# Zero matmuls between the first tiles, a new order of the first loads, and a third PSUM bank for the last gate/up units

## The chip, the cores and the metric

The kernel runs on one core of one Trainium2 chip. The metric is the device time of one execution in microseconds (us); lower is better. Five engines work side by side, each through its own instructions in order: PE (TensorE, the matmuls), ACT (ScalarE), DVE (VectorE), POOL (GpSimd) and SP (SyncE, which here only issues DMAs). They wait for each other and for DMAs through semaphores.

## The reference

A token matrix `x` (2048 x 512, bfloat16) is normalised by rows, and two branches of the result are added to `x`:

```python
xn  = (x - mean) / sqrt(var + 1e-5)                 # by row
# A: linear attention, 32 heads of 16
q, k, v = split(xn @ wqkv)                          # 512 -> 3 * 512
phi(p)  = concat(softmax(p @ w_phi), softmax(-p @ w_phi))     # 16 -> 32 per head
kv = sum_s phi(k)[s]^T v[s];  z = sum_s phi(k)[s]
o  = phi(q) @ kv / (phi(q) @ z + 1e-6)
# B: gated branch, F = 1792
h  = (xn @ w_gate) * (xn @ w_up)
out = x + o @ wo + h @ w_down
```

## The kernel before

The 2048 tokens are 16 tiles of 128 rows. `D = 512` is four blocks of 128 (`NQ`), `F = 1792` is fourteen (`NF`).

**The stages.** For each tile, `emit_ln_stats` (lines 407 to 420) takes mean and variance on DVE (`bn_stats` L410, `bn_aggr` L412), adds epsilon (L417, on DVE for tiles 0 to 3, on POOL for the others), and raises to the power -0.5 on POOL (L419). `emit_xn` (line 433) makes the normalised tile on DVE (L434) and transposes it into `xnT`: for tiles 0 to 3 with four PE matmuls against an identity and an ACT copy (L443, recorded as the helper's L277), for tiles 4 to 15 with a DMA transpose on SP. `k_pe(t)` multiplies a tile by the V weights, `wprime` builds the products W' of the K or Q weights with the feature matrix (its POOL part is `make_wbd`, L392), `k_pk(t)` and `k_norm(t)` make the softmax features of K, `emit_kv` sums K features times V, and `q_pk`, `q_scale`, `q_T` (a DMA transpose), `q_num` (eight narrow matmuls and a division) and `q_oT` (a DMA transpose) do the Q side of one tile. A GLU unit `glu(g, ft)` handles four tiles `g` and one of the fourteen blocks `ft`: four matmuls of 512 columns for the gate into one PSUM bank, four for up into another, an ACT copy of the gate (L543) and a DVE product (L545). There are 56 units; the last nine or ten run among the Q stage. `final(t)` sums 18 matmuls into one bank (the down projection and the attention output), DVE adds `x` (L642), and SP stores the tile.

**Loads.** All come from SP, in the order of the code at lines 352 to 361: tiles 0, 1, 2 and 3 of `x`; the V weights; tiles 4 to 7 of `x`; gate and up columns of blocks 0 to 3; `w_phi`; the K weights, transposed (`load_wT(1, ...)`); gate and up columns of blocks 4 to 13 as one load each, with rows of 2560 bytes. Later loads wait for an earlier DMA.

**Start.** DVE writes a zero tile (L365), and PE runs 46 matmuls of 128 columns on it (line 366) before anything else.

**The order.** The code records steps (`_Sched.step`, `_Sched.dma`) with what they read and write. `_order` (line 732) then plays the steps through with a cost for each, and at each point takes the step that can start first, by priority among those that can start at once. For a load it takes the time `at` as its landing; for a transpose on SP it takes `land` after the start of the issue. The result is one fixed order per engine; the hardware waits for the real semaphores (`_emit_all`). So a changed cost, `at` or `land` changes no instruction, but can change the order on every engine. Every recorded matmul has line L297, every ACT step L277, plain DMAs L165 and DMA transposes L164.

**Banks.** PSUM has eight banks of 512 columns. `a_banks` rotates those of the tile products, `glu_banks` those of the GLU units: (5, 6, 7) first, (4, 5, 6, 7) later, (5, 6) for the last units, and then `final` uses 7 for tiles 0 to 3 and 7, 5, 6 in rotation after that (line 715).

Of the kernel before, what the change touches and what calls it, by code (L numbers as in the profile page):

```python
# [12 lines left out]
PE, ACT, DVE, POOL, SP = "PE", "ACT", "DVE", "POOL", "SP"  # L13
# [7 lines left out]
NQ = D // 128  # L21
# [176 lines left out]
def _build(nc, es, A_x, A_wqkv, A_w_phi, A_wo, B_w_gate, B_w_up, B_w_down, out):  # L198
# [59 lines left out]
    def sbv(name, lo, n):  # L258
        off = layout[name] + lo
        return arena[:, off:off + n]  # L260
# [5 lines left out]
    def bank(b, lo=0, n=512):  # L266
        return psum[:, b * 512 + lo: b * 512 + lo + n]

    sc = _Sched(nc)


    def act_op(out_ap, in_ap, func=ACTF.Copy, scale=1.0, bias=None, prio=None):
        def fn(e):
            kw = {}
            if bias is not None:
                kw["bias"] = bias
            return e.activation(out=out_ap, in_=in_ap, func=func, scale=scale, **kw)  # L277
        r = [in_ap]
        if isinstance(scale, bass.AP):
            r.append(scale)  # L280
        if isinstance(bias, bass.AP):
            r.append(bias)
        return sc.step(ACT, fn, reads=r, writes=[out_ap], cost=(50.0 if str(in_ap.tensor.name) == "ps" else 95.0) + 0.833 * in_ap.free_size(),
                       lat=180.0, prio=prio)

    def dve(fn, reads, writes, n, rate=1.0, fixed=65.0, prio=None):
        return sc.step(DVE, fn, reads=reads, writes=writes, cost=fixed + rate * n / 0.96, lat=150.0, prio=prio)
# [1 line left out]
    def pool(fn, reads, writes, n, rate=1.8, fixed=130.0, prio=None):  # L289
        return sc.step(POOL, fn, reads=reads, writes=writes, cost=fixed + rate * n, lat=120.0, prio=prio)  # L290

    def mms(items, prio=None, warm=False):

        def fn(e):
            ins = None
            for o, l, r, a, z in items:
                ins = e.matmul(o, lhsT=l, rhs=r, start=a, stop=z)  # L297
            return ins
        reads = []
        writes = []  # L300
        c = 0.0
        for o, l, r, a, z in items:
            reads += [l, r]
            writes.append(o)
            c += max(25.0, o.free_size() / 2.4 + 2.3) * (1.6 if warm else 1.0)
        return sc.step(PE, fn, reads=reads, writes=writes, cost=c, lat=260.0, prio=prio)

    def group(o, pairs):
# [3 lines left out]
    ident = sbv("ident", 0, 128)  # L312
# [6 lines left out]
    def x_tile(t):  # L319
        return sbv("x", t * 512, 512)  # L320
# [7 lines left out]
    wv_v = sbv("wv", 0, NQ * 512).rearrange("p (q j) -> p q j", q=NQ)  # L328
# [7 lines left out]
    def load_x(on, t0, n, at):  # L336
        return sc.dma(on, sbv("x", t0 * 512, n * 512).rearrange("p (t d) -> p t d", t=n),
                      x_flat[t0 * 128:(t0 + n) * 128, :].rearrange("(t p) d -> p t d", p=128), at=at)

    def load_w(on, dst, src, at, issue=500.0):  # L340
        return sc.dma(on, dst, src, at=at, issue=issue)

    def load_wT(w, at):

        return sc.dma(SP, wT_v[:, w, :, :], A_wqkv[:, w * 512:(w + 1) * 512], transpose=True, at=at, issue=4600.0)

    def load_gu(on, f0, n, at):
        return [load_w(on, v[:, :, f0 * 128:(f0 + n) * 128],
                       src[:, f0 * 128:(f0 + n) * 128].rearrange("(q p) f -> p q f", p=128), at)
                for v, src in ((wg_v, B_w_gate), (wu_v, B_w_up))]  # L350

    load_x(SP, 0, 1, 3150.0)
    load_x(SP, 1, 1, 3700.0)
    load_x(SP, 2, 2, 4800.0)
    load_w(SP, wv_v, A_wqkv[:, 1024:1536].rearrange("(q p) j -> p q j", p=128), 6800.0)
    load_x(SP, 4, 4, 8200.0)
    load_gu(SP, 0, 4, 10800.0)
    sc.dma(SP, wphi_v, bass.AP(tensor=A_w_phi.tensor, offset=A_w_phi.offset, ap=[[16, 128], [2048, NQ], [1, 16]]),
           at=12500.0)
    load_wT(1, 14500.0)  # L360
    load_gu(SP, 4, 10, 20500.0)


    zero = sbv("tree", 0, 128)
    dve(lambda e: e.memset(zero, 0.0), [], [zero], 128)  # L365
    mms([(bank(7, 0, 128), zero, zero, True, True)] * 46, warm=True)


    def c_fn(e):
# [52 lines left out]
    def xn_tile(t):  # L422
        return sbv("xn", (t % 4) * 512, 512)
# [4 lines left out]
    def next_a():  # L428
        b = a_bank[0] % a_banks[0]
        a_bank[0] += 1  # L430
        return b

    def emit_xn(t):
        dve(lambda e: e.tensor_scalar(out=xn_tile(t), in0=x_tile(t), scalar1=mv_v[:, t, 0:1],  # L434
                                      scalar2=rstd_v[:, t, 0:1], op0=ALU.subtract, op1=ALU.mult),
            [x_tile(t), mv_v[:, t, 0:1], rstd_v[:, t, 0:1]], [xn_tile(t)], 512, rate=0.5)
        if t >= 4:
            sc.dma(SP, xnT_v[:, :, t * 128:(t + 1) * 128], xn_tile(t), transpose=True, issue=1250.0, land=3200.0,
                   at=36000.0 + 1300.0 * (t - 8) if t >= 8 else 22500.0 + 1300.0 * (t - 4))
            return  # L440
        b = next_a()
        mms([(bank(b, q * 128, 128), xn_tile(t)[:, q * 128:(q + 1) * 128], ident, True, True) for q in range(NQ)])
        act_op(xnT_v[:, :, t * 128:(t + 1) * 128], bank(b).rearrange("p (q s) -> p q s", q=NQ))  # L443


# [106 lines left out]
    def emit_kv(half):  # L552
        for g in range(8):
            b = next_a()
            mms(group(bank(b, 0, 65), [(ek_v[:, t, g * 128:(g + 1) * 128], vext_all[:, t, g, 0:65])
                                       for t in range(half * 8, half * 8 + 8)]))
            kp = kvp_v[:, g, :]
            if half == 0:
                act_op(kp, bank(b, 0, 65))
                continue  # L560
            dve(lambda e, b=b, kp=kp: e.tensor_tensor(out=kp, in0=bank(b, 0, 65), in1=kp, op=ALU.add),  # L561
                [bank(b, 0, 65), kp], [kp], 65)
            dve(lambda e, kp=kp, g=g: e.tensor_tensor(
                out=kvx_v[:, g, 0:64].rearrange("p (h d) -> p h d", h=4),
                in0=kp[:, 0:64].rearrange("p (h d) -> p h d", h=4),
                in1=maskh[:, :, None].to_broadcast([128, 4, 16]), op=ALU.mult),
                [kp, maskh], [kvx_v[:, g, 0:64]], 64)
            dve(lambda e, kp=kp, g=g: e.scalar_tensor_tensor(
                out=kvx_v[:, g, 64:68], in0=maskh, scalar=kp[:, 64:65], in1=eps4, op0=ALU.mult, op1=ALU.add),
                [kp, maskh, eps4], [kvx_v[:, g, 64:68]], 4)  # L570


    oT_v = sbv("oT", 0, NQ * S_TOK).rearrange("p (q s) -> p q s", q=NQ)
# [7 lines left out]
    def eq(t):  # L581
        return sbv("eq", (t % 3) * 1024, 1024)

    def eT(t):
        return sbv("eT", (t % 3) * 1024, 1024).rearrange("p (g s) -> p g s", g=8)
# [16 lines left out]
                                      op=ALU.mult), [e1, rs], [e1], 512, rate=0.5)  # L602

    def q_T(t):
        sc.dma(SP, eT(t), eq(t), transpose=True, issue=1250.0, land=3300.0)

    nd = psum[:, 3 * 512:5 * 512].rearrange("p (g k) -> p g k", g=8)

# [11 lines left out]

    def q_oT(t):
        o = sbv("oring", (t % 2) * 512, 512)
        sc.dma(SP, oT_v[:, :, t * 128:(t + 1) * 128], o, transpose=True, issue=1250.0, land=3200.0)


    out_ctr = [0]
# [21 lines left out]
    glu_banks = [(5, 6, 7)]  # L648

    def load_later(*loads):  # L650

        queued = sc.by_eng[SP][-1]
        for load in loads:
            load().deps.append(queued)

    def some_glu(n, g_max):
        for _ in range(n):
            if units and units[0][0] <= g_max:
                glu(*units.pop(0), glu_banks[0])

    def ln(t0, n):
        emit_ln_stats(t0, n)
        for t in range(t0, t0 + n):
            emit_xn(t)
# [9 lines left out]
    for b0 in range(0, NT, 4):  # L674
        if b0 == 4:
            a_banks[0] = 4
            glu_banks[0] = (4, 5, 6, 7)
        if b0 < 12:
            ln(b0 + 4, 4)
        if b0 == 0:  # L680
            load_later(lambda: load_x(SP, 8, 8, 29000.0))
        if b0 == 4:
            load_later(lambda: load_w(SP, wd_v, B_w_down.rearrange("(f p) j -> p f j", p=128), 48000.0),
                       lambda: load_w(SP, wo_v, A_wo.rearrange("(q p) j -> p q j", p=128), 50000.0))
        if b0 == 8:
            load_wT(0, 0.0).deps.append(sc.by_eng[SP][-2])
            emit_kv(0)
            some_glu(99, 2)
        for t in range(b0, b0 + 4):
            k_pk(t)  # L690
            k_norm(t)
            if b0 < 8:
                some_glu(2, 1)
        if b0 < 12:
            for t in range(b0 + 4, b0 + 8):
                k_pe(t)
        if b0 == 8:
            some_glu(4, 3)
            wprime(0)
    emit_kv(1)  # L700
    glu_banks[0] = (5, 6)
    some_glu(99, 3)
    LEAD = 2
    for t in range(NT + LEAD + 1):
# [165 lines left out]
```

## Time and profile before

| | us |
|---|---|
| median of 3 runs | 223.19 (222.98 to 223.47) |
| the profiled execution | 222.43 |
| its span, first to last instruction | 220.7 |
| PE busy in it | 215.4 (98%) |
| DVE busy | 192.8 (87%) |
| ACT busy | 114.4 (52%) |
| POOL busy | 9.6 (4%) |

The lines of a timeline have the start, the length, the engine, the source line, what is written from what, the number of instructions merged into the line and, in brackets, the idle time of the engine before them with what ended it. In the chain of waits each line is a piece of the path that ended last: start, length, who. In a table of stretches the columns are the stretch, its length, PE's busy time with the number of matmuls touched, the granted TensorE clock, the busy share of the DMA engines and GB/s. "PEld" is PE loading a stationary operand. The ends of matmuls are modelled, so neighbouring matmuls overlap in the profile; the spacing of their starts is the real rate.

### The profile page before, as it was taken

How to read it: one execution, taken by the hardware profiler on the slowest of the kernel's cores; microseconds unless marked ns; L12 is line 12 of the kernel's file. 1: busy time of each engine (PE TensorE's matmuls, PEld its weight loads, DVE VectorE, ACT ScalarE, POOL GpSimd, SP SyncE). 2: the span in 40 equal slices, each digit the busy share in tenths (PEclk: the TensorE clock that was granted, in tenths of full speed). 3: DMA queues.
4: the chain of work that ended last, by engine and by line, in shares of the span. 5: the costliest groups of instructions: out<-in, count | busy, mean ns of one | idle time of the engine just before them, and what ended most of it. 6: DMA issues, size and time to landing. Idle time of an engine off the chain costs nothing.

```text
span 220.7 us, 3555 instructions
## 1 busy us (share of the span) xinstructions
PE 215.4 (98%) x1273; PEld 107.0 (48%) x1296; DVE 192.8 (87%) x552; ACT 114.4 (52%) x189; POOL 9.6 (4%) x25
## 2 busy tenths in 40 slices
PE   8899999999999999999999999999999999999995
PEld 8454444444445545444445544444445454444544
DVE  5855999999998289999999999999999999998421
ACT  2668977466442699875543676656454433230000
POOL 4250000200003000000000000000000000000000
PEclk9999999999999999999999999999999999999999
DMA  6999720139200340000000004435446556565621
GB/s 175 324 295 287 177 80 3 25 74 337 88 3 19 77 95 3 0 0 0 3 0 1 3 0 87 79 74 97 95 95 98 117 107 133 77 142 118 99 72 49
DMA packets 46386, 19.91 MB, mean 90 GB/s; under 512 B 37408, under 2 KB 45344, under 8 KB 46368
## 3 DMA queue, kind: packets, MB, share of 16 engines
q1 hardware_dynamic: 46368, 19.68, 38.5%
q8 instruction: 10, 0.16, 0.3%
q14 instruction: 8, 0.07, 0.1%
HBM read 8.67 MB, written 2.10 MB: 49 GB/s over the span
## 4 chain that ended last, share of the span: by engine, by line
PE 94%; DMA 3%; SPq 1%; issue 1%; DVE 1%
PE ps L297 94%; DMA arena<-in_A_x_dram 3%; SPq L165 1%; DVE arena L410 0%; DVE arena L434 0%; DVE arena L642 0%
## 5 line engine op out<-in xcount | busy, mean ns | idle before, releaser
L297 PE MATMUL ps<-arena 128*128 128x512 bf16 (+4 forms) x1273 | 215.4, 331 | 3.0 <-DVE arena L365 1.0
L297 PEld LDWEIGHTS ps<-arena 128*128 128x128 bf16 x1296 | 107.0, 100 | 111.2 <-ACT arena L277 2.2
L277 ACT ACTIVATE arena<-ps 128x512 bf16<-128x512 f32 (+1 forms) x156 | 83.2, 596 | 53.2 <-PE ps L297 45.3
L277 ACT ACTIVATE arena<-arena 128x1024 bf16<-128x1024 bf16 x32 | 34.3, 1082 | 28.2 <-DVE arena L480 25.9
L494 DVE TENSOR_TENSOR arena<-arena 128x512 f32<-128x512 bf16 (+3 forms) x128 | 48.8, 393 | 0.1
L545 DVE TENSOR_TENSOR arena<-ps,arena 128x512 bf16<-128x512 f32 x56 | 38.0, 679 | 3.9 <-ACT arena L277 2.2
L474 DVE TENSOR_TENSOR arena<-arena 128x512 bf16<-128x512 bf16 (+3 forms) x128 | 31.6, 269 | 4.6 <-ACT arena L277 4.4
L480 DVE TENSOR_TENSOR arena<-arena 128x1024 bf16<-128x1024 bf16 x32 | 21.5, 673 | 0.0
L642 DVE TENSOR_TENSOR arena<-ps,arena 128x512 bf16<-128x512 f32 (+2 forms) x17 | 11.1, 651 | 7.4 <-PE ps L297 7.2
L410 DVE BATCH_NORM_STATS2 arena<-arena 128x6 f32<-128x512 bf16 x16 | 10.7, 681 | 1.5 <-DMA arena<-in_A_x_dram 1.5
L521 DVE TENSOR_TENSOR arena<-arena 128x1024 bf16<-128x1024 bf16 x16 | 10.9, 680 | 0.0
L615 DVE TENSOR_TENSOR arena<-ps,arena 128x512 bf16<-128x512 f32 x16 | 10.8, 673 | 0.1
L614 DVE RECIPROCAL arena<-ps 128x32 f32<-128x32 f32 x16 | 5.6, 348 | 3.7 <-PE ps L297 3.5
L518 DVE RECIPROCAL arena<-arena 128x64 bf16<-128x64 f32 x16 | 8.6, 539 | 0.0
L434 DVE TENSOR_SCALAR arena<-arena 128x512 bf16<-128x512 bf16 x16 | 6.1, 406 | 2.2 <-issue 1.5
L601 DVE TENSOR_TENSOR arena<-arena 128x512 bf16<-128x512 bf16 x16 | 6.5, 407 | 0.0
L419 POOL TENSOR_TENSOR arena<-arena 128x1 f32<-128x1 f32 (+1 forms) x7 | 5.3, 764 | 4.1 <-DVE arena L417 3.8
L598 DVE RECIPROCAL arena<-arena 128x32 f32<-128x32 f32 x16 | 5.4, 336 | 0.0
L417 POOL TENSOR_SCALAR arena<-arena 128x4 f32<-128x4 f32 x3 | 1.1, 380 | 55.1 <-DVE arena L412 55.1
L599 DVE TENSOR_TENSOR arena<-arena 128x32 bf16<-128x32 f32 x16 | 2.7, 171 | 0.0
L412 DVE BATCH_NORM_AGGREGATE arena<-arena 128x2 f32<-128x6 f32 x16 | 2.0, 160 | 0.1
L561 DVE TENSOR_TENSOR arena<-ps,arena 128x65 f32<-128x65 f32 x8 | 1.6, 220 | 0.4 <-PE ps L297 0.4
(19 smaller groups left out, 9.8 us busy)
## 6 DMA issues: line engine op xcount, KB each, us to landing
out_dram<-arena SPq DMA_DIRECT2D x15, 128.0 KB, 2.0
arena<-in_B_w_down_dram SPq DMA_DIRECT2D x1, 1792.0 KB, 7.5
arena<-in_B_w_gate_dram SPq DMA_DIRECT2D x1, 1280.0 KB, 6.8
arena<-in_B_w_up_dram SPq DMA_DIRECT2D x1, 1280.0 KB, 10.3
arena<-in_A_x_dram SPq DMA_DIRECT2D x1, 1024.0 KB, 5.4
arena<-arena SPq DMA_TRANSPOSE x44, 2.8
arena<-in_A_wqkv_dram SPq DMA_DIRECT2D x1, 512.0 KB, 4.2
arena<-in_A_x_dram SPq DMA_DIRECT2D x1, 512.0 KB, 5.7
```

The lines of the kernel that those rows point to most:

```text
L277: return e.activation(out=out_ap, in_=in_ap, func=func, scale=scale, **kw)
L297: ins = e.matmul(o, lhsT=l, rhs=r, start=a, stop=z)
L410: dve(lambda e, t=t: e.bn_stats(stats_v[:, t, 0:6], x_tile(t)), [x_tile(t)], [stats_v[:, t, 0:6]], 512)
L474: dve(lambda e, dst=dst, src=src, k=k: e.tensor_tensor(out=dst, in0=src[:, :, 0:k], in1=src[:, :, k:2 * k], op=ALU.max), [src], [dst], 16 ...
L480: dve(lambda e: e.tensor_tensor(out=p4, in0=p4, in1=src[:, :, None, :].to_broadcast([128, 16, 16, 4]), op=ALU.subtract), [pst, src], [pst] ...
L494: dve(lambda e, dst=dst, src=src, k=k: e.tensor_tensor(out=dst, in0=src[:, :, 0:k], in1=src[:, :, k:2 * k], op=ALU.add), [src[:, :, 0:2 * ...
L518: dve(lambda e: e.reciprocal(out=rs, in_=sm), [sm], [rs], 64, rate=6.0)
L521: dve(lambda e: e.tensor_tensor(out=e4, in0=e4, in1=r4[:, :, None, :].to_broadcast([128, 16, 16, 4]), op=ALU.mult), [ek_v[:, t, :], rs], [ ...
L545: dve(lambda e: e.tensor_tensor(out=dst, in0=bank(bu), in1=gr, op=ALU.mult), [bank(bu), gr], [dst], 512, prio=-1.0)
L601: dve(lambda e: e.tensor_tensor(out=e1, in0=e1, in1=rs[:, :, None, :].to_broadcast([128, 8, 16, 4]), op=ALU.mult), [e1, rs], [e1], 512, ra ...
L615: dve(lambda e: e.tensor_tensor(out=o.rearrange("p (g h d) -> p g h d", g=8, h=4), in0=nd[:, :, 0:64].rearrange("p g (h d) -> p g h d", h= ...
L642: dve(lambda e: e.tensor_tensor(out=og, in0=ob, in1=xs, op=ALU.add), [ob, xs], [og], c1 - c0, prio=-2.0)
```

## The change

- The 46 zero matmuls at the start become 39. Seven more are recorded right behind the four transposing matmuls of tile 0, and tied to stand behind them.
- In the loads, the gate and up columns of blocks 0 to 3 are issued before tiles 4 to 7 of `x`.
- The gate and up columns of blocks 4 to 13 come in two portions of five blocks (gate and up of 4 to 8, then of 9 to 13), with rows of 1280 bytes: two more DMA issues on SP.
- Landing times given to the ordering (`at`, `land`) and the cost of cold matmuls change. They add no instruction, but move steps.
- The last GLU units rotate through banks 5, 6 and 7 in place of 5 and 6.

```diff
-    def mms(items, prio=None, warm=False):
+    def mms(items, prio=None, cold=False):
...
-            c += max(25.0, o.free_size() / 2.4 + 2.3) * (1.6 if warm else 1.0)
+            c += max(25.0, o.free_size() / 2.4 + 2.3) * (1.92 if cold else 1.0)
...
-    load_x(SP, 0, 1, 3150.0)
-    load_x(SP, 1, 1, 3700.0)
+    load_x(SP, 0, 1, 2950.0)
+    load_x(SP, 1, 1, 3400.0)
     load_x(SP, 2, 2, 4800.0)
-    load_w(SP, wv_v, A_wqkv[:, 1024:1536].rearrange("(q p) j -> p q j", p=128), 6800.0)
-    load_x(SP, 4, 4, 8200.0)
-    load_gu(SP, 0, 4, 10800.0)
+    load_w(SP, wv_v, A_wqkv[:, 1024:1536].rearrange("(q p) j -> p q j", p=128), 6500.0)
+    load_gu(SP, 0, 4, 9800.0)
+    load_x(SP, 4, 4, 11300.0)
...
-    load_wT(1, 14500.0)
-    load_gu(SP, 4, 10, 20500.0)
+    load_wT(1, 13600.0)
+    load_gu(SP, 4, 5, 17900.0)
+    load_gu(SP, 9, 5, 22300.0)
...
-    mms([(bank(7, 0, 128), zero, zero, True, True)] * 46, warm=True)
+    mms([(bank(7, 0, 128), zero, zero, True, True)] * 39, cold=True)
...
-                   at=36000.0 + 1300.0 * (t - 8) if t >= 8 else 22500.0 + 1300.0 * (t - 4))
+                   at=36000.0 + 1300.0 * (t - 8) if t >= 8 else 22900.0 + 550.0 * (t - 4))
...
-        mms([(bank(b, q * 128, 128), xn_tile(t)[:, q * 128:(q + 1) * 128], ident, True, True) for q in range(NQ)])
+        mms([(bank(b, q * 128, 128), xn_tile(t)[:, q * 128:(q + 1) * 128], ident, True, True) for q in range(NQ)],
+            cold=t < 2)
+        if t == 0:
+            mms([(bank(7, 0, 128), zero, zero, True, True)] * 7, cold=True).deps.append(sc.by_eng[PE][-2])
...
-        sc.dma(SP, eT(t), eq(t), transpose=True, issue=1250.0, land=3300.0)
+        sc.dma(SP, eT(t), eq(t), transpose=True, issue=1250.0, land=4800.0)
...
-        sc.dma(SP, oT_v[:, :, t * 128:(t + 1) * 128], o, transpose=True, issue=1250.0, land=3200.0)
+        sc.dma(SP, oT_v[:, :, t * 128:(t + 1) * 128], o, transpose=True, issue=1250.0, land=4500.0)
...
-            load_later(lambda: load_x(SP, 8, 8, 29000.0))
+            load_later(lambda: load_x(SP, 8, 8, 29800.0))
...
-    glu_banks[0] = (5, 6)
+    glu_banks[0] = (5, 6, 7)
```

## The prediction

> **What bounds the kernel now.** I read the page's first part, then the chain of waits, then the first 30 us of the timeline, stretches of PE and the DMA issues. The page says that PE is the bound:
>
> ```profile
> PE 215.4 (98%) x1273; PEld 107.0 (48%) x1296; DVE 192.8 (87%) x552; ACT 114.4 (52%) x189; POOL 9.6 (4%) x25
> ```
>
> The chain in order of time says where PE could still be helped:
>
> ```profile
> 2.70 5.72 DMA arena<-in_A_x_dram
> 8.42 0.02 issue
> 8.44 0.69 DVE arena L410
> 9.14 0.33 DVE arena L434
> 9.46 0.05 issue
> 9.51 6.47 PE ps L297 x44
> ...
> 146.31 9.27 PE ps L297 x49
> 155.58 0.01 issue
> 155.59 0.43 PE ps L297 x8
> ```
>
> From 9.51 to the last matmul at 218.2 PE hardly pauses: 512-column matmuls start 0.216 us apart, and the only wait I find between the starts is 0.18 before the eight matmuls at 155.59, which follow a DMA transpose. So 209 us are fixed work, and a change can win only ahead of 9.5 us, in that 0.18, or behind 218.2. The path into 9.51 is the load of x 4 to 7, whose statistics (L410, 8.44) stand on DVE ahead of tile 3's normalisation (L434). The timeline of the start:
>
> ```profile
> 4.75 0.38 DVE L434 TENSOR_SCALAR arena<-arena 128x512 bf16<-128x512 bf16 x1
> 5.93 0.38 DVE L434 TENSOR_SCALAR arena<-arena 128x512 bf16<-128x512 bf16 x1
> 6.59 1.09 ACT L277 ACTIVATE arena<-ps 128x512 bf16<-128x512 f32 x2 [4.53 <-PE ps L297]
> 7.47 22.75 PE L297 MATMUL ps<-arena 128*128 128x512 bf16 x119 [0.64 <-ACT arena L277]
> 7.63 0.55 POOL L419 TENSOR_TENSOR arena<-arena 128x1 f32<-128x1 f32 x1 [0.63 <-DVE arena L417]
> 13.51 8.52 SPq L164 DMA_TRANSPOSE arena<-arena  x4
> 22.70 7.24 PEld L297 LDWEIGHTS ps<-arena 128*128 128x128 bf16 x35 [0.31 <-DMA arena<-arena]
> ```
>
> Tile 0 is normalised at 5.13, but PE is in its zero matmuls until 5.92; tile 1 at 6.31; ACT copies tile 0 from 6.59 to 7.19; the V product of tile 0 starts at 7.26 (its first record is missing; its weight load starts at 7.24). The last row shows PE reaching tile 4's V product just as its DMA transpose lands.
>
> ```profile
> 1.20:5.20 4.00, 4.00 (x40) 1.00 0.80 213
> 7.00:9.00 2.00, 1.53 (x11) 1.00 1.05 356
> 15.00:19.00 4.00, 3.95 (x31) 1.00 1.03 386
> ```
>
> Columns: stretch, length, PE busy (matmuls touched), granted clock, DMA share, GB/s. The zero matmuls go at 0.107 us per start; from 6.46 on, 128-column matmuls go at 0.056. The clock column says 1.00 in both, so the spacing, not the column, tells the slow clock.
>
> ```profile
> arena<-in_B_w_gate_dram SPq DMA_DIRECT2D x1, 1280.0 KB, 6.8
> arena<-in_B_w_up_dram SPq DMA_DIRECT2D x1, 1280.0 KB, 10.3
> ```
>
> Issued at 11.28 and 11.89, the big loads land at 18.0 and 22.2, and the four transposes of tiles 4 to 7 land behind them at 22.66, 23.15, 23.64 and 24.09.
>
> **The change, part by part.**
>
> *Zero matmuls and the first tiles.* 46 ended at 5.92; seven fewer end 7 x 0.107 = 0.75 earlier, at 5.17, and tile 0 is ready for PE at 5.13 + 0.055 (the lag of tile 3: DVE end 9.452, matmul 9.509) = 5.19. Its four cold matmuls start the last at 5.51; the copy follows 0.35 later (as 6.24 to 6.59): 5.86 to 6.46, and lets V0 start at 6.52 (lag 0.06). The seven zeros fill PE from 5.62 to 6.36; tile 1 is ready at 6.37 as before, is transposed by 6.67, and V0 starts there: 0.59 earlier. The zeros hold up nobody, since the next matmul waits for DVE until 6.37. V0 to 7.53; tile 2 (ready 7.54) transposed to 7.77; V1 to 8.63.
>
> *x 4 to 7 behind gate and up.* The three loads are 512 KB each and landed at 8.42, 9.93 and 11.40. I take the same slots: gate 8.4, up 9.9, x 4 to 7 at 11.4. In the changed program's order DVE now does tile 3's normalisation ahead of the statistics of tile 4, so it waits only for POOL's power (7.63 + 0.55 = 8.18): it runs 8.28 to 8.66, against 9.05 to 9.45. Transposes 8.72 to 8.94, V2 to 9.80. V3 waits for ACT: evictions and copies start at least 0.49 apart (8.320 to 8.813), so V0 out at 7.73, tile 2's copy 8.22, V1 out 8.83, tile 3's copy 9.32 to 9.92, V3 at 9.98. Before, V3 started at 10.61. **Gain 0.63**, with 0.26 of PE pauses left. Bounds: 0.63 + 0.17 = 0.80 if ACT's order lets V3 follow V2 at once; 0 if the slow clock reaches through V0 (below).
>
> Behind it: unit 0 needs gate at 10.84 and up at 11.70, both there. The statistics of tiles 4 to 7 (four starts 0.6 apart) run 11.4 to 13.9 and stand on DVE ahead of unit 0's product, which ends at 14.5; unit 2 needs that bank at 15.2 (W' at 14.29 plus 0.89). Cover 0.6; a load of x later than 12.0 would cost PE. POOL now builds W' factors (4 x 0.48) ahead of the statistics' power: w_phi lands at 11.6, done 13.5, needed at 14.29. The K weights landed at 13.39. POOL's power for tiles 4 to 7 then ends at 16.3, their normalisation starts at 16.4 instead of 13.06, and SP issues their transposes from 16.9 instead of 13.5. They waited behind the big loads until 22 anyway; that cover holds while those loads are in the queue.
>
> *Two portions.* Two more issues of 0.5 us on SP, after the K weights' and before the transposes; SP is free there until 16.9. The rows halve to 1280 bytes. By the stretches, 1024-byte rows moved at 356 GB/s, 2560-byte rows at 386. So 2.62 MB take 6.8 us at best and 7.4 at worst; nearest is the 1024-byte row, some 7.25: the first transpose lands at 23.13 instead of 22.66. In the new order PE does one more gate group (0.86) ahead of tile 4's V product, so it arrives at 22.73 - 0.63 + 0.86 = 22.96, and 23.13 + 0.07 is **0.24 late**. Bounds 0 (386 GB/s) and 0.34 (356). Tiles 5 to 7 follow 0.49 apart while PE takes 0.86 each: no more waits. x 8 to 15, issued behind the last transpose, land at 30.0 instead of 29.5; DVE wants them at 30.97 - 0.4.
>
> *Third bank and the landing times of the Q stage.* No instruction is added or removed. The last units end ahead of the first `final`, and each `q_num` stands about 1.5 us later behind its transpose than the order allowed before. The 0.18 at 155.4 should go: **gain 0.18**. Against it, DVE (19.8 of 20 us busy in every stretch from 100 to 195) does nine units' products earlier; had PE to wait for one product once, that would be 0.68 (mean of L545). Bounds -0.18 and +0.68; I take -0.18, because PE waited for DVE nowhere in this stage before, with one bank less. At the end, the last `q_num` is followed by 22 + 14 matmuls (7.0 us) before the last transpose is needed; before it landed 4.0 after. Behind 218.2 nothing changes.
>
> Sum: -0.63 + 0.24 - 0.18 = **-0.57** (ends -0.98 and +1.02). The profiled execution took 222.43 (span 220.7), 0.76 under the median 223.19 and below all three runs; I put the difference on the median: 222.6.
>
> **A rule against the change.** In this trace the spacing drops 5.4 us after the first matmul, at 6.46, just before V0. The Trainium skill (TensorE: Matmul & The Clock Gate, Part 1) says that the clock doubles after one full busy window of about 3.4 us, and that the windows run freely, so the moment differs from run to run: by it, an estimate, anywhere from 4.5 to 7.9 here. By the rule the 0.63 would shrink to nothing for the latest moments, since an earlier V0 then runs slowly, and average about 0.5; the sum would be about -0.45 instead of -0.57.
>
> **Rivals.**
> 1. *The start gives nothing (no change).* The switch of the clock falls after V0 starts. Four 512-column matmuls at four times 0.107 each take 1.71 instead of 0.86: V0 6.8 to 8.5, V1 to 9.6, V3 at 10.67. The old kernel had 0.3 of pause ahead of tile 3 to absorb this, the new one none. PE then meets the transposes without waiting: 0.06 - 0.18 = -0.12, 223.1. For it: only one execution shows 6.46. Against: it needs a switch 2 us later. Half of it, or a wait in the Q stage, also ends here.
> 2. *The transposes of tiles 4 to 7 come too late (slower).* Before, their issues took 8.52 us on SP from 13.51 and the last landed 2.07 after its issue. Should they take as long from 16.9, the last lands at 27.5; PE wants it at 22.96 + 3 x 0.86 = 25.55. Price 1.95, sum 1.95 - 0.63 - 0.18 = +1.1, 224.3. It decides from a landing of the last transpose after 26.4. For it: x 4 to 7 come 3 us later, and the big loads are in twice as many rows. Against: the first issue took 1.24 and the stretching looks like waiting for the queue to drain, which does not start anew.
> 3. *The loads lose nothing.* At 386 GB/s the 0.24 goes: -0.81, 222.4. Inside the forecast.
>
> **How the numbers follow.** About 0.2% (0.45 us) is what a measurement of this kernel can tell from no change. Forecast (with rival 3) 0.56: faster by 0.45 or more; its own range 222.3 to 222.75. Rival 1 and its halves 0.28. Rival 2, or a wait of DVE's 0.68 with a late transpose, 0.16. Range 222.2 to 223.5: below it 222.38 less some scatter, above it most of rival 2.
>
> **What would show it.** Right: V0's start at 6.7, V3's at 10.0, no DVE wait for x ahead of tile 3's L434, tile 4's V product at 23.0 to 23.2 with a wait of 0.1 to 0.3, no wait over 0.1 from there to the end, last matmul near 217.7. Wrong: 128- or 512-column matmuls at the slow spacing after 6.7; unit 2 waiting for DVE near 15.2; the first transpose after 23.5 or the last after 25.6; a PE wait for DVE behind 120.

## The result and the profile after

The changed kernel took 222.11 us (median of 12 runs, 221.68 to 222.47), the kernel before 222.80 beside it (222.40 to 223.82): ratio 0.9964, 95% interval 0.9949 to 0.9978. That is 0.69 us faster, and the interval lies below 1 throughout. The profiled execution took 221.73, with a span of 220.0; before it was 222.43 with 220.7. The last matmul starts at 217.487 instead of 218.220, so the span shows a gain of 0.733.

Of the page of the changed kernel, the busy times; then its chain of waits (start, length, who):

```profile
PE 215.1 (98%) x1273; PEld 106.5 (48%) x1296; DVE 192.6 (88%) x552; ACT 113.9 (52%) x189; POOL 9.6 (4%) x25
```

```profile
6.08 0.30 DVE arena L435
6.37 0.07 DVE arena L418
6.45 0.38 PE ps L297 x4
6.83 0.05 issue
6.88 3.13 PE ps L297 x19
10.01 0.04 issue
10.05 5.38 PE ps L297 x36
...
146.20 9.70 PE ps L297 x51
155.90 0.05 issue
155.95 7.79 PE ps L297 x49
```

From 6.45 on, with the transposing matmuls of tile 1, the chain stays on PE (by the starts of its matmuls pauses of 0.08, 0.04 and 0.20 remain, ahead of 7.61, 8.75 and 10.05), and the load of tiles 4 to 7 has left the chain; it used to run into 9.51. V3, the V product of tile 3, starts at 10.05 instead of 10.61: 0.556 earlier. Near 155 PE does not wait any more (before 0.177). 0.556 + 0.177 = 0.733 is the whole difference of the two last matmuls; behind V3 no other wait of PE came or went.

The timeline of the changed kernel, in the same columns as before:

```profile
7.73 2.92 ACT L277 ACTIVATE arena<-ps 128x512 bf16<-128x512 f32 x5 [0.27 <-PE ps L297]
8.28 0.41 DVE L435 TENSOR_SCALAR arena<-arena 128x512 bf16<-128x512 bf16 x1 [0.59 <-POOL arena L420]
16.36 5.83 SPq L164 DMA_TRANSPOSE arena<-arena  x4
21.75 8.58 PE L297 MATMUL ps<-arena 128*128 128x512 bf16 x38
169.08 0.69 DVE L646 TENSOR_TENSOR arena<-ps,arena 128x512 bf16<-128x512 f32 x1 [0.60 <-DMA out_dram<-arena]
```

DVE's normalisation of tile 3 (8.28) waits for POOL's power alone. ACT runs five operations back to back from 7.73 to 10.65; the one that PE needs for V3 ends the last pause of the start (0.20, ahead of 10.05). SP issues the transposes of tiles 4 to 7 from 16.36; they land at 22.68, 23.17, 23.68 and 24.24, and PE goes through the whole stretch from 21.75 without a wait. The last line is new and comes back below: DVE waits for an output store.

How fast the big loads went, from the stretches (columns as before, with the busy times of the other engines in between), and from the issues:

```profile
15.00:19.00 4.00, 3.95 (x25) 1.98 (x24) 2.34 (x6) 3.29 (x7) 0.82 (x1) 1.00 1.06 371
```

```profile
arena<-in_B_w_gate_dram SPq DMA_DIRECT2D x2, 640.0 KB, 6.6
arena<-in_B_w_up_dram SPq DMA_DIRECT2D x2, 640.0 KB, 7.8
```

In this stretch rows of 1280 bytes moved at 371 GB/s, rows of 2560 bytes before at 386. Even so the first transpose landed at 22.68, against 22.66 before. That does not make the two portions free. The K weights, the load just ahead of these on SP, landed at 12.92 in this execution and at 13.39 in the one of before; from there to the landing of the last up columns it took 9.28 here and 8.78 before.

### The profile page after: what moved, and what is told of

It reads as the page before. It is cut to its first block, busy times and chain, and to the rows that moved or that the text cites. A ratio compares the mean times of both kernels' runs of the same rounds, so it can differ in the third digit from the quotient of the medians.

```text
span 220.0 us, 3567 instructions
## 1 busy us (share of the span) xinstructions
PE 215.1 (98%) x1273; PEld 106.5 (48%) x1296; DVE 192.6 (88%) x552; ACT 113.9 (52%) x189; POOL 9.6 (4%) x25
## 4 chain that ended last, share of the span: by engine, by line
PE 95%; DVE 2%; DMA 1%; issue 1%
PE ps L297 95%; DMA arena<-in_A_x_dram 1%; DVE arena L411 1%; DVE arena L435 0%; DVE arena L413 0%; DVE arena L646 0%; DVE arena L418 0%
## 5 line engine op out<-in xcount | busy, mean ns | idle before, releaser
L498 DVE TENSOR_TENSOR arena<-arena 128x64 f32<-128x64 f32 (+3 forms) x128 | 49.1, 394 | 0.1
L277 ACT ACTIVATE arena<-arena 128x1024 bf16<-128x1024 bf16 x32 | 34.5, 1079 | 26.4 <-DVE arena L484 25.8
L411 DVE BATCH_NORM_STATS2 arena<-arena 128x6 f32<-128x512 bf16 x16 | 10.7, 682 | 3.1 <-DMA arena<-in_A_x_dram 3.1
```

The lines of the kernel that those rows point to most:

```text
L411: dve(lambda e, t=t: e.bn_stats(stats_v[:, t, 0:6], x_tile(t)), [x_tile(t)], [stats_v[:, t, 0:6]], 512)
L498: dve(lambda e, dst=dst, src=src, k=k: e.tensor_tensor(out=dst, in0=src[:, :, 0:k], in1=src[:, :, k:2 * k], op=ALU.add), [src[:, :, 0:2 * ...
```

## Experiments

Of all these kernels, timed values are medians of runs with the kernel before on the same chip, whose median was 222.71 to 222.89 each time. None of them leaves out part of the computation: the zero matmuls feed nothing.

### Which part moves the start

Three kernels add parts of the new start to the kernel before, and one takes the new end from the changed kernel.

`a1`, the zeros alone (with the cost that the change gives to cold matmuls):

```diff
-    mms([...] * 46, warm=True)
+    mms([...] * 39, cold=True)
+        if t == 0:
+            mms([...] * 7, ...)      # behind tile 0's transposing matmuls
```

> The kernel before with its 46 zero matmuls split into 39 and 7; loads, landing times, portions and banks as before, and no other step of any engine moves. Theory (the zeros and the order of the loads gain only together): V0 starts near 6.7 instead of 7.26, but tile 3's normalisation still waits on DVE for x 4 to 7 (landing 8.4), so V3 starts at 10.6 and the time is that of before, within 0.1 us. Rival (the zeros in front were the whole loss): V3 0.55 earlier, and the time 0.5 lower or, if tile 4's transpose then holds PE, 0.1 lower with a wait of 0.5 at 22.2.

Measured: 222.87 against 222.78, ratio 1.0004 (0.9991 to 1.0018). In its timeline V0, the V product of tile 0, starts 0.3 earlier (the V weights landed at 6.82 and held it to 6.95), but tile 3 still waits:

```profile
8.36 0.69 DVE L410 BATCH_NORM_STATS2 arena<-arena 128x6 f32<-128x512 bf16 x1 [0.73 <-DMA arena<-in_A_x_dram]
8.97 0.40 DVE L434 TENSOR_SCALAR arena<-arena 128x512 bf16<-128x512 bf16 x1
```

```profile
9.42 1.91 PE L297 MATMUL ps<-arena 128*128 128x128 bf16 x11 [0.35 <-DVE arena L434]
```

The statistics of tile 4 hold DVE until 8.97, V3 starts at 10.52 (before 10.61), and the last matmul at 218.205. What the zeros gain is lost at the next wait.

`a2`, the load order alone, and `a3`, both:

```diff
-    load_x(SP, 4, 4, 8200.0)
-    load_gu(SP, 0, 4, 10800.0)
+    load_gu(SP, 0, 4, 9800.0)
+    load_x(SP, 4, 4, 11300.0)
```

> The kernel before with gate and up columns loaded ahead of x 4 to 7; 46 zeros in front, one portion, old landing times of the transposes, old banks. Theory: tile 3 is normalised by 8.7, but V0 waits for the zeros. With the clock's switch at 6.46, as in the first profile of before, V0 at 7.26 and V3 at 10.55; with a switch near 5.45, as in the profile of the changed kernel, the 46 zeros end sooner and V3 comes near 10.1. PE then waits at tile 4's V product for a transpose that lands near 22.7, so the time is that of before within 0.1 either way. Rival (the order of the loads alone carries the gain): 0.5 lower.

> Both together, without the portions, the landing times and the third bank: PE takes tile 4's V product where it did before, with no gate group ahead of it. Theory: V3 at 10.05 as in the changed kernel, PE reaches tile 4's V product 0.5 earlier, at 22.2, and waits there 0.5 for the transpose that lands near 22.7; the time is 0 to 0.1 below before. Rival (the start alone gives the gain): 0.5 to 0.6 below before.

Measured: `a2` 222.46, ratio 0.9993 (0.9975 to 1.0011); `a3` 222.46, ratio 0.9985 (0.9969 to 1.0001). V3 starts at 10.38 and at 10.04: with both parts the start is as early as in the changed kernel. But PE then comes to tile 4's V product before its transpose. In `a3`:

```profile
22.74 3.63 PE L297 MATMUL ps<-arena 128*128 128x512 bf16 x16 [0.41 <-DMA arena<-arena]
```

The transpose landed at 22.69; from start to start PE lost 0.574 there, and the last matmul is at 218.244, where it was before. A gain of 0.57 at 10 us was given back in full at 22.

`a5`, the changed kernel with the old end:

```diff
-    glu_banks[0] = (5, 6, 7)
+    glu_banks[0] = (5, 6)
-        sc.dma(SP, eT(t), ..., land=4800.0)
+        sc.dma(SP, eT(t), ..., land=3300.0)
-        sc.dma(SP, oT_v..., o, ..., land=4500.0)
+        sc.dma(SP, oT_v..., o, ..., land=3200.0)
```

> The changed kernel with two banks and the old landing times of the Q stage: all of the change but its tail. Theory: V3 at 10.05, one gate group ahead of tile 4's V product, no wait at 22.8, and in the Q stage a wait of 0.1 to 0.3 for a transpose as before: 0.4 to 0.6 below before. Rival (the gain is made in the Q stage by the third bank): the time of before, within 0.2.

Measured: 222.34, ratio 0.9986 (0.9969 to 1.0002). V3 at 9.99; PE has the extra gate group ahead of tile 4's V product and arrives at 22.76. In this execution the transpose landed at 23.31, so 0.376 was lost there, and 0.185 near 155. Last matmul 218.007. It was expected to wait nowhere at 22.8, and did. By these traces the start is a chain of three: zeros, load order, and a group of matmuls put ahead of tile 4's V product; without the third the gain at 10 is lost at 22, with it the loss depends on the landing. The timings don't separate the parts: the ratios of `a3` and `a5` are 0.9985 and 0.9986, and both intervals reach 1.

### One portion or two

`b4`: the changed kernel with gate and up of blocks 4 to 13 as one load each.

```diff
-    load_gu(SP, 4, 5, 17900.0)
-    load_gu(SP, 9, 5, 22300.0)
+    load_gu(SP, 4, 10, 20500.0)
```

> The changed kernel with gate and up columns of blocks 4 to 13 as one load each (rows of 2560 bytes), every other step in its place on every engine. My prediction's price of the halved rows: the first transpose of tiles 4 to 7 lands 0.4 earlier than with two portions. Its rival, from the profile of the changed kernel, where it landed at 22.68 with halved rows: the same landing within 0.2. But the gate columns of unit 4 are taken ahead of tile 4's V product and the single load lands near 18, which is in time. Either way the time is that of the changed kernel within 0.2, unless the first transpose lands after 22.8.

Measured: 222.13, ratio 0.9969 (0.995 to 0.9987), the same as the changed kernel. Its first transpose landed at 23.60, later than the changed kernel's 22.68 with half rows. But in that execution the whole queue was late: the V weights landed at 7.16 and the K weights at 14.29, against 6.49 and 12.92. Counted from the landing of the K weights, in us:

| kernels | to the last up columns |
|---|---|
| rows of 2560 bytes: before, `a1`, `a2`, `a3`, `b1`, `b4` | 8.78, 8.75, 8.85, 9.05, 8.70, 8.82 |
| rows of 1280 bytes: the changed kernel, `a4`, `a5`, `b2`, `b3`, `d2`, `d3`, `e1` to `e4` | 9.28, 9.62, 9.61, 9.46, 9.50, 9.68, 9.50, 9.81, 9.58, 9.34, 9.52 |
| rows of 1280 bytes: `c1` | 8.29 |

So two portions with half rows took longer: 0.46 between `b4` and the changed kernel, which differ in nothing else, and 0.71 between the means of the first two rows. Whether the rows or the two more loads do it was not tried. `c1` is an exception with a likely cause, which comes with the zeros below. The moment of the landing varies between executions by as much again, since the K weights landed anywhere from 12.92 to 14.47. The late V weights cost `b4` its start as well: V0 had to wait for them, and V3 started at 10.58, so that PE came to the transposes late and lost only 0.08 there.

### The end

`b1`, the new end alone on the kernel before; `b2`, the changed kernel with two banks; `b3`, the changed kernel with the old landing times:

```diff
# b1: before
+    land=4800.0 / 4500.0, glu_banks[0] = (5, 6, 7)
# b2: after
-    glu_banks[0] = (5, 6, 7)
+    glu_banks[0] = (5, 6)
# b3: after
-    land=4800.0 / 4500.0
+    land=3300.0 / 3200.0
```

> The kernel before with the third bank for the last units and the later landing times of the Q stage, nothing else of the change. Theory: the start is that of before (V3 at 10.6), the wait of 0.18 near 155 goes, no other comes, the last matmul starts 0.18 earlier (218.04 against 218.22), the time is 0.1 to 0.2 lower. Rival (DVE, busy in this stage, holds PE once): a PE wait for DVE of up to 0.7 after 120 and a time above that of before.

> The changed kernel with banks 5 and 6 alone for the last units, the later landing times kept. Theory (the landing times remove the wait, the bank does not): no wait of PE for a transpose after 120, last matmul near 217.5. Rival (the third bank removes it): a wait of 0.1 to 0.3 for a transpose or for DVE between 125 and 160.

> The changed kernel with landing times 3.3 and 3.2 for the Q stage, three banks kept. Theory: PE waits again for a transpose, 0.1 to 0.4 in total after 120, last matmul 217.6 to 217.9. Rival (the third bank removes the wait): none, 217.5.

Measured: `b2` 222.57 and `b3` 222.68, one run each. With two banks and late landings PE waits for DVE twice, about 0.175 at 139.6 and 0.086 at 144.1; with three banks and early landings it waits 0.145 for a transpose at 195.3. In one execution of each, only the two together leave no wait in this stage. `b1` took 222.70 against 222.89, ratio 0.9996 (0.9971 to 1.0021), too wide to show 0.18. In its profiled execution (224.05, with tile 1 of `x` and the V weights 0.6 and 1.1 us later than in the profile of before, which explains its start) the wait at 155 is gone and another stands at 174. Its chain:

```profile
168.32 3.67 DMA out_dram<-arena
172.08 0.69 DVE arena L642
...
174.04 0.60 DVE arena L615
174.65 0.11 DVE arena L474
174.79 0.42 PE ps L297 x8
```

DVE's final addition (L642) waited for a store, the division of a `q_num` (L615) behind it came late, and PE lost 0.667. The next group explains the store.

### The zeros, and a detour

`c1`: one zero matmul in all. `a4`: 39 ahead of the first tile, none in the pause.

```diff
# both
-        if t == 0:
-            mms([...] * 7, cold=True).deps.append(sc.by_eng[PE][-2])
# c1 also
-    mms([...] * 39, cold=True)
+    mms([...] * 1, cold=True)
```

> The changed kernel with one zero matmul in place of 46. It prices the slow clock by itself. Theory: PE first works at 5.2, the spacing drops some 3.2 to 5.4 later (the spread of the profiles so far, counted from the first matmul), between 8.4 and 10.6; V0 takes 1.7 instead of 0.86, V1 up to 1.7, and V3 starts between 10.7 and 12. The time is 0.5 to 1.5 above the changed kernel's, less if tile 4's transpose is late anyway. Rival (the start waits for loads and DVE in any case): V3 at 10.1 to 10.5, a time within 0.3 of the changed kernel's.

> The changed kernel with 39 zero matmuls in front and none in the pause of tile 0. Theory: the seven hold nobody up and speed up nobody, because in most profiles the spacing has already dropped to 0.056 before the pause; PE stands idle from about 5.6 to 6.4, V0 and V3 start as in the changed kernel, the time is that of the changed kernel within 0.15. Rival (the pause keeps the clock slow): 128-column matmuls 0.107 apart or 512-column ones 0.43 apart after 6.7, and a time 0.3 to 1 above the changed kernel's.

Measured: `c1` 224.17, ratio 1.0069 (1.0049 to 1.009). PE's stretches of `c1`, then of the changed kernel (the number in brackets is the matmuls touched):

```profile
7.00:9.00 2.00, 2.00 (x10) 1.00 1.07 365
9.00:11.00 2.00, 2.00 (x9) 1.00 1.37 291
```

```profile
7.00:9.00 2.00, 2.00 (x16) 1.00 1.09 354
9.00:11.00 2.00, 1.96 (x12) 1.00 1.20 267
```

Without the zeros the 512-column matmuls start 0.43 apart until 11.54, and 0.216 apart from 11.77 on; V2 starts at 11.12 and V3 at 12.20, 2.15 behind the changed kernel's 10.05, and so do ACT's evictions, which follow PE. V3 was expected between 10.7 and 12, and the time 0.5 to 1.5 above the changed kernel's; it is 2.06 above. So the zeros ahead of the data are what the start rests on.

`a4` took 223.11, ratio 1.0021 (1.0001 to 1.004), 221.83 to 224.18: 1 us slower than the changed kernel. That looked like a proof that PE must not pause in the start. Its trace says otherwise: the spacing drops at 5.29, V3 starts at 10.01, as early as with the zeros. The losses are 0.418 for tile 4's transpose (it landed at 23.38), and behind that, from the timeline:

```profile
171.24 0.69 DVE L644 TENSOR_TENSOR arena<-ps,arena 128x512 bf16<-128x512 f32 x1 [2.37 <-DMA out_dram<-arena]
...
173.95 1.28 PE L297 MATMUL ps<-arena 128*128 128x68 bf16 x12 [0.93 <-DVE arena L476]
```

This is the wait of `b1` again, and the 0.60 at 169.08 of the changed kernel is its small form. The code explains it. In the changed order DVE does the final addition of tile 4 ahead of that of tile 3. The staging buffer has two halves that alternate by tile, so tile 4 writes the half that tile 2's store is still reading. Before, tile 3 and its half came in between. The store was issued at 167.05 and landed 4.09 later (in the changed kernel 2.32; most stores 1.7). DVE's delay of 2.37 became 1.09 of PE at 172.9, and another 0.49 at 193 for a transpose that followed late.

And why was the store late here? The page has an instruction queue, q8, with ten packets of 16 KB over the span. By the trace's packet records one of them started at 169.03 in `a4`, at 166.87 in the changed kernel. From the DMA view of `a4` (168.5 to 169.9) and of the changed kernel (166.5 to 168.0), packets, MB and share of 16 engines:

```profile
q8 instruction: 1, 0.02, 4.3%
```

```profile
q8 instruction: 1, 0.02, 3.8%
```

In `a4` the 256-byte packets that started right behind it, at 169.1 to 169.3, took 1.7 to 1.9 us each; in the changed kernel none from 166 to 172 took over 0.4. The kernel without the seven matmuls has a program that is seven matmuls shorter on PE, so PE comes to the same place in the order with fewer instructions behind it, and the packet later. The traces bear this out: in all eighteen this packet, the eighth, starts when PE has done 847 to 868 of its weight loads, one for each matmul, whether that is at 165.97 (`a5`) or at 176.15 (`c1`, 45 matmuls shorter). This made two theories that four more kernels could separate: "pause" (PE's idle time itself costs) and "store".

```diff
# e1: after, shorter by seven elsewhere; the pause keeps its seven
-    mms([...] * 39, cold=True)
+    mms([...] * 32, cold=True)
# e2: a4 with the halves of tiles 3 and 4 exchanged; e3: the same on after
-        i = out_ctr[0]
+        i = out_ctr[0] + (t in (3, 4))
```

> The changed kernel with 32 zero matmuls ahead of the first tile instead of 39; the seven in the pause stay. Theory 'store': without the seven in the pause the kernel took 223.1 because PE's program was seven matmuls shorter: a 16 KB packet on the instruction queue came at 169.03 instead of 166.87, onto the store of tile 2, which landed 4.09 us after its issue instead of 2.32, held DVE's final addition of tile 4 (same half of the staging buffer) for 2.37 us and then PE for 1.09 at 172.7. Here the program is just as short, so that packet comes at 168.5 to 169.1, DVE waits 1.5 to 2.5 us for the store, and the time is 222.7 to 223.2. Theory 'pause': PE must not pause in the start; with the zeros in the pause kept, the time is that of the changed kernel, 221.9 to 222.3, and V3 starts at 10.05 by both.

> The changed kernel without the seven zero matmuls in the pause, and with the staging halves of tiles 3 and 4 exchanged, so that the final addition of tile 4 waits for the store of tile 1 (long landed) and that of tile 3 for the store of tile 2. Theory 'store': the late store holds nobody up, DVE has no wait over 0.3 near 169, PE none over 0.2 at 172, and the time falls from 223.1 to 221.9 to 222.3. Theory 'pause': it stays at 222.9 to 223.2.

> The changed kernel with the staging halves of tiles 3 and 4 exchanged. Theory 'store': the 0.60 us that DVE waits for the store at 168.5 go; in the profiled execution PE did not wait for it, so the gain is in other executions alone: 221.8 to 222.1, less scatter. Theory 'pause': no difference from 222.1.

Measured: `e1` 223.61, ratio 1.0029 (1.001 to 1.0048), above the 222.7 to 223.2 of theory "store"; `e2` 222.12, ratio 0.9969 (0.9952 to 0.9986); `e3` 221.94, ratio 0.9964 (0.9949 to 0.9979). With the pause filled and the program short, the loss is there; with the pause empty and the halves exchanged, it is gone. `e1`'s packet came at 168.47, within the 168.5 to 169.1 expected but for 0.03, and its timeline has

```profile
171.41 0.69 DVE L646 TENSOR_TENSOR arena<-ps,arena 128x512 bf16<-128x512 f32 x1 [2.13 <-DMA out_dram<-arena]
```

and a PE loss of 0.848 at 173. In `e2` the store was late too (issued at 167.57, landed 3.29 later), but nobody waited:

```profile
166.86 0.69 DVE L644 TENSOR_TENSOR arena<-ps,arena 128x512 bf16<-128x512 f32 x1
168.58 0.69 DVE L644 TENSOR_TENSOR arena<-ps,arena 128x512 bf16<-128x512 f32 x1
```

Its profiled execution (222.62) lost only 0.927 at 22.8, to a transpose that landed at 23.88. So "pause" falls, and with it my reading of `a4`: the seven zeros in the pause are not needed for the clock. What they do is to make the program long enough that the packet starts 0.21 behind the store's issue in the changed kernel, and not 1.0 to 2.0 as in `a4`, `e1` and `e2`, and that is luck. That the shorter program and the shared half make the loss is shown by `e1` and `e2`; that the q8 packet itself slows the packets behind it is argued from the order of events in the traces of `a4` and `b1` (there 169.84, and packets of 1.3 to 1.4 us from 170.4 on) and of the kernel before (166.82, and 0.8 to 1.0 us from 167.9 on), and was not tried by itself. All eighteen traces agree with it: of 306 output stores, 42 have such a packet starting between 0.4 us ahead of their issue and their landing, and among these are all 17 that took over 3.2 us and 26 of the 30 over 2.5; the median of the others is 1.74. It also fits the exception of `c1` above: there no such packet starts while the big loads run (the first comes at 24.99), in every other kernel one does (17.4 to 20.2). `e3` is 0.17 below the changed kernel's median, but its ratio to the kernel before is the same, 0.9964: where the packet comes early on the store, the shared half costs nothing that the runs can show.

### A better version

The changed kernel still leans on the landing of tile 4's transpose. `d3` puts a second group of matmuls (unit 4's up) ahead of tile 4's V product on PE. `d2` also puts ACT's copy of tile 3 ahead of the eviction of V1. `e4` is `d3` with the halves exchanged.

```diff
# d3, d2, e4: PE's finished order; step 35 is unit 4's up group, step 27 tile 4's V product
+    up = on_pe.pop(35)
+    on_pe.insert(27, up)
# d2: ACT's order
+    on_act[4], on_act[5] = on_act[5], on_act[4]      # V1's eviction, tile 3's copy
```

> The changed kernel with one step of PE moved: the up group of unit 4 stands ahead of tile 4's V product, behind its gate group, so PE reaches that product 0.86 later, near 23.7. In the profiles so far that have the same front, the first transpose landed between 22.7 and 23.8 and PE waited 0 to 0.64 for it. Theory: the wait goes, the time is 0.1 to 0.5 below the changed kernel's, 0.8 to 1.1 below before. Rival (the K products come 0.86 later and DVE, full from 20 on, gives it back): no gain, or a wait for DVE between 30 and 60.

> As the one above, and on ACT tile 3's copy stands ahead of the eviction of V1. Theory: V3 follows V2 at once and starts 0.2 earlier than in the changed kernel, near 9.85 where the V weights are in time; with the cover ahead of tile 4 the 0.2 stays: another 0.1 to 0.2 below the run above. Rival (the V weights' landing or tile 3's normalisation sets V3): no difference from the run above.

> The kernel with unit 4's up matmuls ahead of tile 4's V product (221.67 before), and the staging halves of tiles 3 and 4 exchanged. Theory 'store': DVE's wait of 0.38 for the store goes, PE waits nowhere behind 10.05 as before: 221.5 to 221.7. Theory 'pause': 221.7, no difference.

Measured: `d3` 221.67 (221.57 to 221.95), ratio 0.9959 (0.9942 to 0.9975); `d2` 221.71 (221.43 to 222.40), ratio 0.9960 (0.9947 to 0.9973); `e4` 221.69, ratio 0.9959 (0.9943 to 0.9975). The whole chain of `d3`:

```profile
0.78 0.09 issue
0.87 0.12 DVE arena L366
0.99 0.05 issue
1.04 8.97 PE ps L297 x74
10.01 0.04 issue
10.05 207.67 PE ps L297 x1222
217.72 0.02 issue
217.74 0.29 DVE arena L646
```

From 10.05 to the end nothing releases PE but PE, though in this execution the first transpose landed at 23.42, 0.6 after the changed kernel asks for it. In `d2` V3 follows V2 at once, at 9.83, so the 0.2 of ACT's order is real; in the profiled execution it was lost again (0.504 at 32.1 for DVE, whose statistics waited for `x` 8 to 15, landed at 31.49, and 0.23 near 74), and the medians don't differ. In the profiled execution of `e4` (222.48) the V weights landed at 7.39 and V3 started at 10.82. `d3` and `e4` are the best timed, 0.44 and 0.42 under the changed kernel's own measurement; against the changed kernel the intervals overlap.

## Why the prediction was right or wrong

The forecast was faster, at 222.6 with a range from 222.2; it came out faster, at 222.11, below the range. The sum, -0.57, stands against -0.69 between the medians and -0.733 between the last matmuls. The terms below are measured in one profiled execution of each kernel; how the 0.69 of the medians divides among them is not shown.

**The step that failed** is "I put the difference on the median: 222.6". The median of three runs, 223.19, was a high one: the three are among the 12 beside the changed kernel, whose median is 222.80 (222.61 for the other nine), and later sets have 222.71 to 222.89. That is 0.39 of the miss of 0.49; the rest is the sum, -0.57 against -0.69. The profiled execution, which the prediction noted to be "below all three runs", was 0.37 below 222.80, within the spread of the executions. The low end, "222.38 less some scatter", stands on the same 223.19 and so was 0.39 too high. Put on 222.80, the sum gives 222.23.

**The start, -0.63.** Measured -0.556. Most steps held: V0 near 6.67 (predicted 6.67), tile 3's normalisation at 8.28 (8.28), V2 at 8.99 (8.94), V3 at 10.05 (9.98), ended by ACT. The seven zeros did not fill the pause: they ran 0.056 apart from 5.54, not 0.107 apart, and PE stood idle until 6.43. The traces of `a1`, `a2` and `a3` show that both the zeros and the load order are needed for it (V3 0.09, 0.23 and 0.57 earlier than before); the prediction had this as two paragraphs of one sum and did not say that either alone gives little. It also put the landing of the V weights at nothing. V0 follows it by 0.13 in `a1` and `b4`, so V0 holds the forecast of 6.67 only where they are there by about 6.5. They landed at 6.49 here, but at 6.92, 7.16 and 7.39 in the profiled executions of `b3`, `b4` and `e4`, and V3 started at 10.34, 10.58 and 10.82.

**The transposes, +0.24.** Measured 0 in the profiled execution. The price of the two portions, some 0.45 for their rows, was right or low: 0.46 between `b4` and the changed kernel, 0.71 between the means. What failed was to hang it on the K weights of one execution, 13.39; in the profiled execution of the changed kernel they landed 0.47 earlier, and the two cancelled. Elsewhere PE did arrive before tile 4's transpose: 0.376 in `a5`, 0.418 in `a4`, 0.642 in `b2`, 0.495 in `b3`, 0.738 in `e1`, 0.927 in `e2`. It is a term of 0 to 0.9 by the execution, and the upper bound of 0.34 was too low. An estimate of its size in the medians is 0.44, by which `d3`, where PE asks for that transpose 0.86 later, is below the changed kernel. Rival 3 gave the size of the profiled execution by luck: the loads did lose by the two portions.

**The end, -0.18.** Right for the profiled execution: 0.177 gone, no wait in its place. A wait for DVE like that of the upper bound, 0.68, also exists: 0.667 in `b1`, 0.848 in `e1`, 1.09 in `a4`. The cause is not the one I wrote. I argued from banks and from DVE's load (19.5 to 19.9 of 20 us, not 19.8 in every stretch); it is the final addition of tile 4, which the new order brings forward onto a staging half whose store is under way. The prediction compared the place of the `q_num`s in the two orders and not that of the `final`s.

**Rival 1, the clock.** It did not happen. The spacing changed at 5.43 in the changed kernel, and in all kernels with 32 or more zeros between 3.99 and 6.56, which is 2.9 to 5.5 us after the first matmul (in the profile of before the first short gap starts at 6.556, not at 6.46); only `b1` lies a little later, at about 6.6. It was not far away: in `d3` the spacing changed at 6.50, 0.17 ahead of V0, and the start lost nothing. The Trainium skill (TensorE: Matmul & The Clock Gate, Part 1) has a free-running window of about 3.4 us and the doubling after one busy one, an estimate of 3.4 to 6.8 after the first matmul; the spread of the runs agrees but for its early end, where the earliest (2.95 in `e2`) lies 0.5 below it. `c1`, where PE takes up steady work at 5.27 and the spacing changes at 11.54, shows what a late change costs: V3 2.15 later.

**Rival 2, the transposes 2 us late.** It did not happen: the four issues took 5.83 instead of 8.52, and the last transpose landed at 24.24, 2 us ahead of the 26.4 that decides (26.24 in `e2`, the latest of all traces).

## What to carry over

A gain ahead of a load or a transpose is kept only if there is other work to put in front of the next thing that lands: in the traces the zeros and the load order bring V3 0.57 earlier together, and without a moved group of matmuls all of it is given back at tile 4's transpose. To see what a load costs, count from the landing of what stands ahead of it in the queue, over several executions, and not by the clock of one: by the clock the two portions looked free. When a scheduler's costs are changed, compare the order of every buffer's users, not only of the steps that the change names; two steps that trade places can meet in a ring of two. And put a predicted difference on as many runs as there are of the old kernel, with the profiled execution as a second anchor, since three runs can lie 0.4 us off.

## What the runs showed of the hardware

The landing of the same load moves between executions by more than the effects studied here: the V weights, with the same loads ahead of them in all eighteen kernels, landed at 6.2 to 7.5. Tile 4's transpose, behind loads whose order and rows differ, landed at 22.2 to 23.9.

While the program runs, 16 KB packets arrive on an instruction queue every 17 to 27 us, ten in the span, and their moments go by the program and not by the clock: 166.87 in the changed kernel, 169.03, 168.47 and 168.61 in `a4`, `e1` and `e2`, which are seven matmuls shorter. Where one starts 0.9 to 2.0 us behind the issue of the output store near 167, 256-byte packets right behind it take up to 1.9 us and the store 3.2 to 4.1 instead of 1.7. Seven matmuls that compute nothing made 1.5 us between the medians of `e1` and the changed kernel; in the profiled execution of `e1` PE loses 0.848 at 173 behind the late store, and 0.549 at 194.

The granted clock reads 1.00 from the first slice on, in `c1` too, where 512-column matmuls start 0.43 apart; only the spacing shows the slow phase.
